# Seven half-width products in place of eight for two thirds of an expert layer's blocks (linear attention, then hash-routed experts)

## The chip, the cores and the metric

One core of one Trainium2 chip runs the whole kernel in one launch. The metric is the device time of that launch in microseconds (us), the median of several runs. Every matrix and every product is float32. The engines are named as the profile names them: PE (matrix products; PEld is its loading of weights), DVE (vector), ACT (activation), POOL (general, here the one that scatters rows) and SP (issues the loads).

## The reference

```python
def _attn_ref(q, k, v, beta):                      # (4, 8, 768, 48)
    k_n = k / (np.linalg.norm(k, axis=-1, keepdims=True) + 1e-06)
    state = np.zeros((B, H, D, D))
    for t in range(S):
        kt, vt, bt = (k_n[:, :, t], v[:, :, t], beta[:, :, t, None])
        y[:, :, t] = np.einsum('bhd,bhde->bhe', q[:, :, t], state)
        v_old = np.einsum('bhde,bhd->bhe', state, kt)
        state = state + bt[:, :, :, None] * np.einsum('bhd,bhe->bhde', kt, vt - v_old)
    return y

def _moe_ref(x, token_ids, w1, w2):                # x: y as (3072, 384); w1 (8, 384, 1024); w2 (8, 1024, 384)
    expert_idx = token_ids * np.int64(2654435761) % np.int64(E)
    for e in range(E):
        mask = expert_idx == e
        h = np.maximum(x[mask] @ w1[e], 0.0)
        out[mask] = h @ w2[e]
    return out
```

## The kernel before

**First part, the attention.** The 768 tokens of a sequence are taken in 24 chunks of 32, for all 32 heads at once. `chunk(c)` is the recurrence; DVE inverts a triangular matrix for each group of four chunks (`inverse`). A list scheduler (`order()`) with estimated costs sets the order of this part's instructions. At the end of a chunk ACT copies the finished rows out of PSUM into `x_sb` (L695), and POOL scatters them to a DRAM scratch, sorted by expert.

**Second part, the experts.** The experts are sorted by their number of tokens and called e0 to e7 here (the largest is e0). Each has a fixed width, `WIDTHS` = 424, 424, 392, 392, 380, 380, 366, 366 columns (tokens); what is over goes through a loop at the end that runs as often as the data ask. 288 columns of e0 (`EARLY`) are computed ahead, at the end of the first part; its other 136 (`LATE`) open the second part's loop. This part's order is the order of the code (`tc.manual_schedule()`), engine by engine.

- `fetch(e)` and `weights(e)` issue the loads on SP's queue: rows from the scratch, `w1` and `w2` of an expert (1536 KB each). `w_pool2` has three buffers of each weight; e4 takes e0's place (`w_first`).
- `turn(e, i)`: DVE transposes the rows in 32x32 blocks, with a stride of three, to `xT`, whose 384 input features lie as three blocks of 128 (index `co` or `i`).
- `gemm1` (L1186): the first product. For each of 8 blocks of 128 hidden features (`fo`), three matrix products (one for each `co`) of the full width add up in one PSUM bank; ACT (L1189) and DVE (L1191) take turns at clearing negative values on the way to `h_sb`.
- `turned` (L1216): the second product of e0 to e6. For each of three output blocks `i`, eight products (one for each `fo`); the weights are `w2[:, fo, i::CO]`, so every third column. DVE transposes the bank to `o_sb` (L1219), and `scatter` (L1224) sends it out, one indirect DMA of POOL for each 32 tokens.
- `direct` (L1199): the second product of e7, with tokens on the partitions, in three pieces of 122 tokens; then a copy (L1203) and a scatter (L1205).

A float32 product shows up in the trace as two passes, each with a weight load and a matmul: a row with x48 stands for 24 products. e0's late 136 columns use a copy of its `w2` with contiguous columns (`w2_runs`, made by ACT at L1252); all the other `turned` products load strided weights.

## Time and profile before

| what | value |
|---|---|
| median of 3 runs | 483.76 us (483.18 to 486.18) |
| the profiled execution: time, span in the trace | 486.72 us, 485.1 us |
| PE busy | 440.3 us (91%), 6544 matmuls |
| PEld busy | 335.5 us (69%) |
| DVE busy | 249.5 us (51%) |
| ACT busy | 170.5 us (35%) |
| POOL busy | 175.0 us (36%) |
| mean granted TensorE clock | 0.952 of full speed |

Busy time is a share of the whole span, which has two very different parts. The first ends at about 221 us; the second is read by itself. The profiled execution's time is 1.62 us more than its span, and 2.96 us above the median of the runs.

### The profile page before, as it was taken

What the parts mean: (1) busy time and instruction counts of PE and PEld (TensorE: products, weight loads), DVE (VectorE), ACT (ScalarE), POOL (GpSimd) and SP (SyncE); (2) the same over time, 40 slices, a digit from 0 to 9 for tenths busy, and PEclk for the clock granted to TensorE, in tenths of its full rate; (3) what the DMA queues carried; (4) which work ended last, traced back from release to release, by engine and by line L of the source; (5) the groups of instructions that cost most, each with busy time, mean ns of one, the idle gap of its engine ahead of it and who ended that gap; (6) DMA issues with size and microseconds to landing.
All of it is one profiled execution on the core that took longest, in us unless ns stands there. A gap on an engine that the chain in (4) does not pass through costs nothing. (4 is left out here: it accounts for less than half of the span.)

```text
span 485.1 us, 15906 instructions
## 1 busy us (share of the span) xinstructions
PE 440.3 (91%) x6544; PEld 335.5 (69%) x6544; DVE 249.5 (51%) x903; ACT 170.5 (35%) x361; POOL 175.0 (36%) x231
## 2 busy tenths in 40 slices
PE   6798898989988977789999999999999999999991
PEld 4675787877767876677896665766767767677650
DVE  6799899999999799981222121221212112121100
ACT  3569876858866566455000001001000010000100
POOL 9671323214131251532056007427054170541710
PEclk8759799989998899899999999999999999999997
DMA  8994646556573373544998237064090460000100
GB/s 128 148 154 110 113 86 131 108 102 122 105 133 83 97 163 80 106 168 114 317 311 251 94 59 282 22 201 157 10 321 29 100 255 3 24 23 7 38 32 16
DMA packets 98009, 58.28 MB, mean 120 GB/s; under 512 B 84262, under 2 KB 91953, under 8 KB 97168
## 3 DMA queue, kind: packets, MB, share of 16 engines
q1 hardware_dynamic: 88640, 39.67, 34.8%
q0 software_dynamic: 8016, 17.27, 13.2%
q8 instruction: 52, 0.85, 0.8%
q10 hardware_dynamic: 1280, 0.32, 0.3%
q14 instruction: 21, 0.17, 0.1%
HBM read 44.51 MB, written 10.65 MB: 114 GB/s over the span
## 5 line engine op out<-in xcount | busy, mean ns | idle before, releaser
L1224 POOL DMA_INDIRECT out_dram<-o_sb,idx x81 | 79.3, 979 | 123.1 <-DVE o_sb L1219 100.4
L1186 PE MATMUL h_ps<-xT,w_sb 128*128 128x392 f32 (+3 forms) x288 | 94.5, 488 | 0.0
L1189 ACT ACTIVATE h_sb<-h_ps 128x392 f32<-128x392 f32 (+4 forms) x32 | 14.9, 466 | 211.4 <-PE h_ps L1186 211.4
L1186 PEld LDWEIGHTS h_ps<-xT,w_sb 128*128 128x128 f32 x288 | 54.6, 190 | 38.2 <-issue 7.6
L1216 PE MATMUL o_ps<-h_sb,w_sb 128*128 128x392 f32 (+3 forms) x240 | 79.6, 491 | 0.0
L1216 PEld LDWEIGHTS o_ps<-h_sb,w_sb 128*128 128x128 f32 x240 | 60.3, 251 | 18.8 <-issue 0.2
L1191 DVE TENSOR_SCALAR h_sb<-h_ps 128x392 f32<-128x392 f32 (+4 forms) x32 | 16.9, 527 | 95.9 <-PE h_ps L1186 95.9
L700 POOL DMA_INDIRECT x_scratch<-x_sb,slot x24 | 25.9, 1078 | 104.1 <-ACT x_sb L695 34.1
L1219 DVE STREAM_TRANSPOSE o_sb<-o_ps 128x384 f32<-128x384 f32 (+4 forms) x24 | 16.1, 669 | 84.7 <-PE o_ps L1216 84.7
L571 DVE TENSOR_TENSOR U<-U,tmp 128x30 f32<-128x30 f32 (+9 forms) x180 | 58.1, 323 | 0.0
L567 DVE TENSOR_TENSOR tmp<-U,Ni 128x30 f32<-128x30 f32 (+9 forms) x180 | 57.9, 322 | 0.1
L602 PE MATMUL bank<-S,KQ 128*32 128x96 f32 x1472 | 38.6, 261 | 4.7 <-ACT S L748 4.0
L563 DVE SCALAR_TENSOR_TENSOR U<-U,Ni 128x1 f32<-128x1 f32 (+30 forms) x186 | 42.4, 228 | 0.2
L748 ACT ACTIVATE S<-psS 48x768 f32<-48x768 f32 x43 | 34.6, 806 | 19.0 <-PE psS L670 15.6
L602 PEld LDWEIGHTS bank<-S,KQ 128*32 128x32 f32 x1472 | 33.4, 117 | 8.7 <-ACT S L748 5.8
L670 PE MATMUL psS<-W,K 32*112 32x96 f32 x736 | 26.9, 275 | 8.7 <-ACT W L660 5.5
L641 PE MATMUL bank<-W,MT 64*64 64x48 f32 x768 | 30.3, 231 | 2.0 <-issue 1.5
L670 PEld LDWEIGHTS psS<-W,K 32*112 32x112 f32 x736 | 22.2, 178 | 12.1 <-ACT W L660 7.4
L641 PEld LDWEIGHTS bank<-W,MT 64*64 64x64 f32 x768 | 26.8, 145 | 4.9 <-issue 2.4
L506 POOL DMA_DIRECT2D Tz<-TU x24 | 17.6, 741 | 29.3 <-ACT Tz L951 12.7
L335 POOL DMA_DIRECT2D Q<-in_q_dram x40 | 23.0, 583 | 6.1 <-PE early L370 4.2
L489 ACT ACTIVATE MT<-GQ,kmask 128x256 f32<-128x256 f32 x48 | 22.3, 512 | 0.0
(167 smaller groups left out, 588.5 us busy)
## 6 DMA issues: line engine op xcount, KB each, us to landing
w_sb<-in_moe_w_dram SPq DMA_DIRECT2D x12, 1536.0 KB
V<-in_v_dram SPq DMA_DIRECT2D x96, 48.0 KB
K<-in_k_dram SPq DMA_DIRECT2D x89, 48.0 KB
Q<-in_q_dram SPq DMA_DIRECT2D x56, 48.0 KB
xr<-x_scratch SPq DMA_DIRECT2D x16, 145.5 KB
Tz<-TU POOLq DMA_DIRECT2D x24, 96.0 KB, 3.3
Q<-in_q_dram POOLq DMA_DIRECT2D x40, 48.0 KB, 4.4
w_first<-in_moe_w_dram POOLq DMA_DIRECT2D x3, 512.0 KB, 5.0
```

The source lines that it names most:

```text
L335: eng].dma_start(out=dst[quarter(b)],
L563: nc.vector.scalar_tensor_tensor(out=U[:, n, 0:n], in0=U[:, j, 0:n], scalar=Ni[:, j, n:n + 1], in1=U[:, n, 0:n], op0=ALU.mult, op1=ALU.add)
L567: nc.vector.tensor_tensor(t, U[:, j:n, 0:n].to_broadcast([P, m, n]), Ni[:, j, n + 1:, None].to_broadcast([P, m, n]), op=ALU.mult)
L571: nc.vector.tensor_tensor(U[:, n + 1:, 0:n], U[:, n + 1:, 0:n], t, op=ALU.add)
L602: nc.tensor.matmul(res[quarter(b), u], lhsT=KQ[:, u, a, quarter(b)], rhs=S0[:, b, u].rearrange("p r d -> p (r d)"), start=(a == 1 and u == ...
L641: nc.tensor.matmul(to[rows, h], lhsT=lhsT(rows, h), rhs=rhs[rows, h], start=(first and h == 0), stop=True, skip_group_check=True, tile_pos ...
L670: nc.tensor.matmul(late["S"][0:DP + D, b, 2 * D * u:2 * D * u + 2 * D], lhsT=K4[quarter(b), u].rearrange("p r d -> p (r d)")[:, 0:DP + D], ...
L700: put = nc.gpsimd.indirect_dma_start(out=x_dram[:, :], out_offset=bass.IndirectOffsetOnAxis(ap=slot[:, c:c + 1], axis=0), in_=x_sb.rearran ...
L748: put = nc.scalar.activation(S1[half(r), :, :, r], new[half(r), :, :, r], ACT.Copy)
L1186: nc.tensor.matmul(h_ps[:, :width], lhsT=w1_sb[:, co, fo * P:(fo + 1) * P], rhs=xT[:, co, :width], start=(co == 0), stop=(co == CO - 1))
L1216: nc.tensor.matmul(os_ps[i][:, 0:width], lhsT=w2_sb[:, fo, i::CO] if runs is None else runs[:, fo, i], rhs=h_sb[:, fo, 0:width], start=(fo ...
L1224: scat = nc.gpsimd.indirect_dma_start(out=out_q, out_offset=bass.IndirectOffsetOnAxis(ap=of[:, k:k + 1], axis=0), in_=o_sb[:, k], in_offse ...
```

## The change

For e1 to e7 two of the three blocks of the first product's contraction (`co` 0 and 1) are no longer multiplied out as 2 x 2 block products of half the columns. The weights are cut in 2 x 2 blocks (hidden features f and f+4 against `co` 0 and 1), the tokens in two halves, and each set of eight half-width products is replaced by seven, of sums and differences of the blocks (Winograd's form of Strassen's method): DVE makes the sums of weights and columns beforehand (`sums1`), and DVE and ACT join the products out of four half banks. The third block (`co` 2) is multiplied as before, in halves. The same is done in the second product of e1 to e5, with output blocks 0 and 1 against hidden blocks f and f+4 (`seven2`, `sums2_weights`, `sums2_columns`); output block 2 keeps its eight full-width products there. e0's products, e6's second and e7's second product keep their form; e7's are put in another order, and its result is copied in two halves, by ACT and by DVE.

In the loop e's first product now stands ahead of (e-1)'s second, and e0's late second product behind e1's first. The sums for an expert stand on DVE one stage ahead. `w_pool2` has two buffers; e0's place takes e3 and e6. The load of an expert's `w1` is issued three experts ahead, as soon as its place is free, that of its `w2` two ahead. In the first part the rows are laid out differently: ACT's copy to `x_sb` reads PSUM with a stride of three, and DVE's transposes to `xT` read contiguous rows.

```diff
-                x_sb[:, :, 0:DQ], flat_y.rearrange("p (q y) -> p q y", q=QN), ACT.Copy, scale=-1.0))
+                x_sb[:, :, 0:DQ].rearrange("p q (i r) -> p q i r", i=CO),
+                flat_y.rearrange("p (q r i) -> p q i r", q=QN, i=CO), ACT.Copy, scale=-1.0))
...
-    with tc.tile_pool(name="w_pool2", bufs=3) as w_pool2, \
+    with tc.tile_pool(name="w_pool2", bufs=2) as w_pool2, \
...
+        banks = [ps_m.tile([P, BANK], F32, name=f"bank{i}") for i in range(8)]
+        os_ps, hs_ps, t_ps = banks[0:3], banks[3:6], banks[6]
+        HF, HB, HC = F // 2, FO // 2, CAP // 2
+        two = itertools.cycle([(banks[i], banks[i + 1]) for i in range(0, 8, 2)])
...
+        def sums_of_weights(s, a11, a12, a21, a22):
+            return [plus(s[0], a21, a22), minus(s[1], s[0], a11), minus(s[2], a11, a21),
+                    minus(s[3], a12, s[1])]
+
+        def sums_of_columns(t, b11, b12, b21, b22):
+            return [minus(t[0], b12, b11), minus(t[1], b22, t[0]), minus(t[2], b22, b12),
+                    minus(t[3], b21, t[1])]
...
+        def seven1(e, h_sb, others):
...
+            def first(f):
+                used[f], part[f] = next(two), next(parts)
+                al, be, de, ep = halves_of(used[f], n)
+                blk = slice(f * P, f * P + P)
+                mm(al, a(0, f), x[:, 0, 0:n], True)
+                mm(be, s[1][:, blk], t[1][:, 0:n])
+                mm(ep, s[2][:, blk], t[2][:, 0:n], True)
+                mm(de, s[0][:, blk], t[0][:, 0:n])
+                mm(de, a(2, f + HB), x[:, 2, n:2 * n])
+                p0, p1 = (p[:, 0:n] for p in part[f])
+                nc.scalar.copy(p1, al)
+                run([plus(p0, p1, be), plus(p1, p0, ep), plus(h_sb[:, f + HB, n:2 * n], p1, de)])
+
+            def second(f):
...
+                mm(al, a(1, f), x[:, 1, 0:n])
+                mm(al, a(2, f), x[:, 2, 0:n])
+                mm(ep, a(1, f + HB), t[3][:, 0:n])
+                mm(ep, a(2, f + HB), x[:, 2, 0:n])
+                mm(de, s[3][:, blk], x[:, 1, n:2 * n])
+                mm(de, s[4][:, blk], x[:, 2, n:2 * n])
+                p0 = part[f][0][:, 0:n]
+                nc.scalar.activation(h_sb[:, f, 0:n], al, ACT.Relu)
+                run([plus(h_sb[:, f + HB, 0:n], p0, ep)])
+                nc.scalar.activation(h_sb[:, f + HB, 0:2 * n], h_sb[:, f + HB, 0:2 * n], ACT.Relu)
+                run([plus(h_sb[:, f, n:2 * n], p0, de)])
+                nc.scalar.activation(h_sb[:, f, n:2 * n], h_sb[:, f, n:2 * n], ACT.Relu)
+
+            for what, f, k in ((first, 0, 2), (first, 1, 1), (first, 2, 1), (second, 0, 1),
+                               (first, 3, 1), (second, 1, 1), (second, 2, 1)):
+                what(f)
+                run(others, k)
+            run(others)
+            second(3)
+
+        def seven2(e, h_sb, o_sb, befores, others):
...
+            for fo in range(FO):
+                mm(third[:, 0:2 * n], of_out(w2[:, fo], 2), h_sb[:, fo, 0:2 * n], fo == 0)
+            for f in range(HB):
+                mm(al, of_out(w2[:, f], 0), h_sb[:, f, 0:n], f == 0)
+            for f in range(HB):
+                mm(be, s[1][:, f], t[1][:, f, 0:n])
...
+            run(befores)
+            nc.scalar.copy(oT[2][:, 0:2 * n], third[:, 0:2 * n])
+            turn_out(e, o_sb, 2)
+            nc.scalar.copy(p1, al)
+            run([plus(p0, p1, be)])
+            run(others, 1)
+            run([plus(p1, p0, ep)])
+            run(others, 1)
+            run([plus(oT[1][:, n:2 * n], p1, de)])
+            run(others)
+            for f in range(HB):
+                mm(al, of_out(w2[:, f + HB], 0), h_sb[:, f + HB, 0:n])
+            for f in range(HB):
+                mm(ep, of_out(w2[:, f + HB], 1), t[3][:, f, 0:n])
...
+            for e in range(1, E - 1):
+                hs[e] = m_h.tile([P, FO, CAP], F32, name="h_sb")
...
+                seven1(e, hs[e], others)
...
+                    turns_of_rows(e + 1)
+                    o_sb = m_o.tile([P, NB_MAX, DQ], F32, name="o_sb")
+                    others = sums2_columns(e, hs[e]) if e < E - 2 else []
+                    seven2(e - 1, h_sb, o_sb, sums1(e + 1),
+                           (sums2_weights(e) if e < E - 2 else []) + others[:2])
+                    del others[:2]
+                    scatter(idx[e - 1], o_sb, range(NBS[e - 1]))
+                if e + 2 < E:
+                    weights2(e + 2)
+                if e + 3 < E:
+                    fetch(e + 3)
+                    weights1(e + 3)
...
```

PE, at e2's last first-product blocks and the second product that follows them, before (`h_ps` and `o_ps` are PSUM banks; x3 and x8 count products, of 392 columns):

```order
L1186 MATMUL h_ps_4962<-xT,w_sb 128x392 x3
L1186 MATMUL h_ps_4963<-xT,w_sb 128x392 x3
L1216 MATMUL o_ps_4958<-h_sb,w_sb 128x392 x8
L1216 MATMUL o_ps_4959<-h_sb,w_sb 128x392 x8
L1216 MATMUL o_ps_4960<-h_sb,w_sb 128x392 x8
```

The same place on PE now: `second(3)` of e2's first product, then e1's second product (`h_first` holds its sums of weights, `h_sums` its sums of columns):

```order
L1169 MATMUL bank_4964<-xT,w_sb 128x196 x2
L1169 MATMUL bank_4965<-x_sum_4978,w_sb 128x196
L1169 MATMUL bank_4965<-xT,w_sb 128x196
L1169 MATMUL bank_4965<-xT,w_sum_4969 128x196
L1169 MATMUL bank_4965<-xT,w_sum_4970 128x196
L1169 MATMUL bank_4960<-h_sb,w_sb 128x424 x8
L1169 MATMUL bank_4958<-h_sb,w_sb 128x212 x4
L1169 MATMUL bank_4958<-h_sums,h_first 128x212 x4
L1169 MATMUL bank_4959<-h_sums,h_first 128x212 x8
L1169 MATMUL bank_4958<-h_sb,w_sb 128x212 x4
L1169 MATMUL bank_4959<-h_sums,w_sb 128x212 x4
L1169 MATMUL bank_4959<-h_sb,h_first 128x212 x4
```

Half-width products stand where full-width ones stood, and the last three rows add to half banks that DVE and ACT must first have read.

DVE during e2's second product, before (`xT<-xr` turns the next expert's rows, `o_sb<-o_ps` the results):

```order
L1191 TENSOR_SCALAR h_sb<-h_ps_4963 128x392
L1166 STREAM_TRANSPOSE xT<-xr 128x416
L1219 STREAM_TRANSPOSE o_sb<-o_ps_4958 128x416
L1166 STREAM_TRANSPOSE xT<-xr 128x416
L1219 STREAM_TRANSPOSE o_sb<-o_ps_4959 128x416
```

DVE during e1's second product now (`w_sum` and `x_sum` above the `o_sb` row are e3's, for the first product that follows; `w_sum_4971` and later are e2's, for its second product; `part` and `oT` join e1's):

```order
L1155 TENSOR_TENSOR w_sum_4970<-w_first 128x512
L1286 STREAM_TRANSPOSE o_sb<-oT_4990 128x448
L1158 TENSOR_TENSOR part_4980<-part_4981,bank_4958 128x212
L1158 TENSOR_TENSOR w_sum_4971<-w_sb 128x512
L1158 TENSOR_TENSOR part_4981<-part_4980,bank_4959 128x212
L1155 TENSOR_TENSOR w_sum_4972<-w_sum_4971,w_sb 128x512
L1158 TENSOR_TENSOR oT_4989<-part_4981,bank_4959 128x212
L1155 TENSOR_TENSOR w_sum_4973<-w_sb 128x512
```

The reads of `bank` that release PE's last three rows now stand behind three transposes and nine sums, and between further sums.

## Rows read from the trace of the kernel before

**Rows 1.** PE in order of time: start us, us, line, operation; x48 is 24 products

```profile
200.65 1.14 PE L641 MATMUL pair<-R,Tz 64*64 64x48 f32 x32 [1.96 <-DVE Tz L499]
...
233.57 11.95 PE L1216 MATMUL o_ps<-h_first,w_first 128*128 128x288 f32 x48 [0.60 <-issue]
245.35 5.72 PE L1186 MATMUL h_ps<-xT,w_first 128*128 128x136 f32 x48
250.91 5.72 PE L1216 MATMUL o_ps<-h_sb,w_runs 128*128 128x136 f32 x48
256.47 17.24 PE L1186 MATMUL h_ps<-xT,w_sb 128*128 128x424 f32 x48
273.55 17.24 PE L1216 MATMUL o_ps<-h_sb,w_sb 128*128 128x424 f32 x48
290.63 15.96 PE L1186 MATMUL h_ps<-xT,w_sb 128*128 128x392 f32 x48
306.43 15.96 PE L1216 MATMUL o_ps<-h_sb,w_sb 128*128 128x392 f32 x48
...
429.87 14.92 PE L1216 MATMUL o_ps<-h_sb,w_sb 128*128 128x366 f32 x48
444.63 14.92 PE L1186 MATMUL h_ps<-xT,w_sb 128*128 128x366 f32 x48
```

**Rows 2.** Busy time by stage: PE, PEld, DVE, ACT, POOL; then clock, DMA, GB/s

```profile
180.00:200.00 20.00, 14.98 (x512) 13.09 (x500) 19.89 (x79) 12.42 (x30) 5.01 (x7) 1.00 0.35 83
...
233.50:245.40 11.90, 11.83 (x49) 11.81 (x50) 1.14 (x2) 0.00 (x0) 0.00 (x0) 1.00 1.11 322
245.40:256.40 11.00, 11.00 (x97) 11.00 (x96) 4.58 (x12) 1.13 (x4) 7.86 (x8) 1.00 0.78 289
...
290.00:322.00 32.00, 32.00 (x99) 21.45 (x98) 6.39 (x11) 1.99 (x4) 13.71 (x14) 1.00 0.44 137
```

**Rows 3.** PE's weight loads by form, 270 to 486 us: busy us, mean ns

```profile
L1216 PEld LDWEIGHTS o_ps<-h_sb,w_sb 128*128 128x128 f32 x240 | 60.3, 251 | 18.8 <-issue 0.2
L1186 PEld LDWEIGHTS h_ps<-xT,w_sb 128*128 128x128 f32 x249 | 47.3, 190 | 32.1 <-issue 1.7
...
L1199 PEld LDWEIGHTS o_ps<-w_sb,h_sb 128*122 128x122 f32 x48 | 8.9, 185 | 6.6
```

**Rows 4.** DVE by form, 300 to 486 us: busy us, mean ns of one

```profile
L1166 DVE STREAM_TRANSPOSE xT<-xr 128x384 f32<-128x384 f32 x12 | 7.9, 658 | 0.0
...
L1191 DVE TENSOR_SCALAR h_sb<-h_ps 128x392 f32<-128x392 f32 x6 | 3.4, 566 | 20.1 <-PE h_ps L1186 20.1
```

**Rows 5.** DVE by form, 200 to 262 us

```profile
L1191 DVE TENSOR_SCALAR h_sb<-h_ps 128x136 f32<-128x136 f32 x4 | 1.2, 299 | 4.1 <-PE h_ps L1186 4.1
```

**Rows 6.** DVE in order of time, 212 to 290 us

```profile
212.07 0.38 DVE L769 TENSOR_TENSOR rt<-rt,iota_f 128x216 f32<-128x216 f32 x1
212.49 0.38 DVE L769 TENSOR_TENSOR rt<-rt,rt 128x216 f32<-128x216 f32 x1
```

**Rows 7.** ACT by form, 200 to 262 us

```profile
L1252 ACT COPY w_runs<-w_first 128x384 f32<-128x384 f32 x8 | 5.1, 709 | 2.3 <-DMA x_scratch<-x_sb,slot 2.3
...
L695 ACT ACTIVATE x_sb<-bank 128x384 f32<-128x384 f32 x4 | 2.0, 491 | 2.6 <-PE bank L641 1.5 <-issue 1.1
...
L1189 ACT ACTIVATE h_sb<-h_ps 128x136 f32<-128x136 f32 x4 | 1.1, 284 | 17.6 <-PE h_ps L1186 17.6
```

**Rows 8.** ACT in order of time, the last chunks of the first part

```profile
217.84 0.55 ACT L632 ACTIVATE R<-bank 128x192 f32<-128x192 f32 x2 [0.57 <-PE bank L602]
```

**Rows 9.** SP's queue in order of time: the issue of e1's `w1`

```profile
230.05 0.36 SPq L80 DMA_DIRECT2D w_sb<-in_moe_w_dram  x1
```

**Rows 10.** The end of the kernel, in order of time

```profile
475.11 0.48 ACT L1203 COPY last_o<-o_ps 122x384 f32<-122x384 f32 x1 [9.83 <-PE o_ps L1199]
475.86 0.98 POOL L1205 DMA_INDIRECT out_dram<-last_o,last_i  x1 [4.07 <-POOLq L1286]
```

More of the change, by code (lines that the diff above doesn't have):

```diff
@@ new lines, with minus, plus @@
+        w2_runs = h_all[:, 0:FO * CO * P].rearrange("p (o i d) -> p o i d", o=FO, i=CO)
+        parts = itertools.cycle([[m_l.tile([P, HC], F32, name=f"part{i}{k}") for k in range(2)]
+                                 for i in range(4)])
+        oT = [m_l.tile([P, NB_MAX * TB], F32, name=f"oT{i}") for i in range(CO)]
+        def minus(out, a, b):
+            return lambda: nc.vector.tensor_tensor(out, a, b, op=ALU.subtract)
+        def plus(out, a, b):
+            return lambda: nc.vector.tensor_tensor(out, a, b, op=ALU.add)
@@ new lines, in seven2 @@
+        def seven2(e, h_sb, o_sb, befores, others):
+            w2, s, t, n = w_tiles[e][1], w2_sums[e % 2], h_sums, WIDTHS[e] // 2
+            pair, (third, _) = next(two), next(two)
+            al, be, de, ep = halves_of(pair, n)
+            p0, p1 = (p[:, 0:n] for p in next(parts))
+            for fo in range(FO):
[5 more added lines that the diff above has]
+            for f in range(HB):
+                mm(ep, s[2][:, f], t[2][:, f, 0:n], f == 0)
+            for f in range(HB):
+                mm(de, s[0][:, f], t[0][:, f, 0:n])
+            run(befores)
[8 more added lines that the diff above has]
+            run(others)
+            for f in range(HB):
+                mm(al, of_out(w2[:, f + HB], 0), h_sb[:, f + HB, 0:n])
+            for f in range(HB):
+                mm(ep, of_out(w2[:, f + HB], 1), t[3][:, f, 0:n])
+            for f in range(HB):
+                mm(de, s[3][:, f], h_sb[:, f + HB, n:2 * n])
+            nc.scalar.copy(oT[0][:, 0:n], al)
+            run([plus(oT[1][:, 0:n], p0, ep)])
+            turn_out(e, o_sb, 1)
+            run([plus(oT[0][:, n:2 * n], p0, de)])
+            turn_out(e, o_sb, 0)
@@ L1228, in scatter, with weights1, weights2, turns_of_rows @@
                 tc.add_to_no_dep_group("scatters", scat.ins)
[L1230 to L1236 removed]
+        def weights1(e):
+            w1 = moe_w1[bass.ds(regs[1][e], 1)].rearrange("o d f -> (o d) f")
+            home = w_tiles[0][0] if e % 3 == 0 else w_pool2.tile([P, CO, F], F32, name="w1_sb")
+            nc.sync.dma_start(out=home, in_=w1.rearrange("(p co) f -> p co f", p=P))
+            w_tiles[e] = home, None
+        def weights2(e):
+            w2 = moe_w2[bass.ds(regs[1][e], 1)].rearrange("o f d -> (o f) d")
+            home = w_tiles[0][1] if e % 3 == 0 else w_pool2.tile([P, FO, DIN], F32, name="w2_sb")
+            nc.sync.dma_start(out=home, in_=w2.rearrange("(fo p) d -> p fo d", p=P))
+            w_tiles[e] = w_tiles[e][0], home
+        def turns_of_rows(e):
+            for i in range(CO):
+                turn(e, i)
+            places(e)
         with tc.manual_schedule():
@@ L1240 @@
             fetch(1)
-            weights(1)
+            weights1(1)
+            weights2(1)
+            turns_of_rows(0)
+            n_ov = nc.values_load(ov_i[0:1, NOV:NOV + 1], min_val=0, max_val=NOV)
+            fetch(2)
+            weights1(2)
+            weights2(2)
             w1_sb, w2_sb = w_tiles[0]
-            for i in range(CO):
-                turn(0, i)
-            places(0)
             o_sb = m_o.tile([P, NB_MAX, DQ], F32, name="o_sb")
+            turns_of_rows(1)
+            soon = sums1(1)
+            run(soon, 3)
             for i in range(CO):
                 turned(w2_sb, first["h"], o_sb, i, EARLY, 0)
+                run(soon, 3 if i < CO - 1 else None)
             scatter(idx_first, o_sb, range(EB))
-            w2_runs = m_l.tile([P, FO, CO, P], F32, name="w2_runs")
-            for fo in range(FO):
-                nc.scalar.copy(w2_runs[:, fo], w2_sb[:, fo].rearrange("p (d i) -> p i d", i=CO))
+            fetch(3)
+            for t in oT:
+                nc.vector.memset(t, 0.0)
             nc.vector.memset(last_i, BIG)
@@ L1286 @@
+            e = E - 2
+            o_sb = m_o.tile([P, NB_MAX, DQ], F32, name="o_sb")
+            os_ps = [next(two)[0] for _ in range(CO)]
+            for i in range(CO):
+                turned(w_tiles[e][1], hs[e], o_sb, i, WIDTHS[e], 0)
+            scatter(idx[e], o_sb, range(NBS[e]))
+            hs[e + 1] = m_h.tile([P, FO, CAP], F32, name="h_sb")
+            seven1(e + 1, hs[e + 1], [])
+            direct(w_tiles[e + 1][1], hs[e + 1])
         with tc.For_i(0, n_ov, 1) as it:
@@ L1315 @@
             gemm1(w1_sb, xT, h_sb, P)
-            direct(w2_sb, h_sb, 0, P, to[:, 0:1], False)
+            for fo in range(FO):
+                nc.tensor.matmul(os_ps[0][:, 0:DIN], lhsT=h_sb[:, fo, 0:P], rhs=w2_sb[:, fo, :],
+                                 start=(fo == 0), stop=(fo == FO - 1))
+            last(os_ps[0], P, 0, to[:, 0:1])
 _INS = ['q', 'k', 'v', 'beta', 'moe_token_ids', 'moe_w1', 'moe_w2']
```

150 lines of the change are left out of this document (94 added, 56 removed).

## The prediction

> **What bounds the kernel now.** I read the stages first, then PE in order of time, then the loads and the helpers by form. From 245 us on PE is busy all the time, at a granted clock of 1.00, the 2.4 GHz level; DVE is busy 6.4 us of 32 and ACT 2.0 [rows 2]. PE's rows follow each other without a gap [rows 1], so in the second part a column of PE work saved is time saved, as long as nothing new holds PE up. The length of a pass comes from the starts: 48 passes of 392 columns take 306.43 - 290.63 = 15.80 us, 329.2 ns each; of 424 columns 17.08 us, 355.8 ns; of 366 columns 14.76 us, 307.5 ns; of 136 columns 5.56 us, 115.8 ns [rows 1]. All four lie on 0.833 ns a column plus 2.5 ns. By that line 380 columns take 319.2 ns, and halves take 179.2 (212 columns), 165.8 (196), 160.8 (190) and 155.0 ns (183).
>
> **First products of e1 to e7.** A first product was 24 full-width products, 48 passes. Now each of four blocks has 5 products in `first` and 6 in `second`, so 44 of half width, 88 passes: 88 x 179.2 = 15.77 us for 17.08; 14.59 for 15.80 (e2, e3); 14.15 for 15.32 (e4, e5); 13.64 for 14.76 (e6, e7). Gains: 1.31 + 2 x 1.21 + 2 x 1.17 + 2 x 1.12 = 8.3 us.
>
> **Second products of e1 to e5.** Eight full products stay (16 passes), 28 half ones follow (56 passes). 16 x 355.8 + 56 x 179.2 = 15.73 us for 17.08 (e1); 14.55 for 15.80 (e2, e3); 14.11 for 15.32 (e4, e5). Gains: 1.35 + 2 x 1.25 + 2 x 1.21 = 6.3 us. The columns together: **14.6 us**. e0's, e6's second and e7's second products keep their passes.
>
> **Weight loads under shorter passes.** Loads overlap the pass before. A contiguous load is recorded with 190 ns [rows 3], yet 96 passes of 136 columns go at 115.8 ns with PEld busy throughout [rows 1, 2]: at least 74 ns of the record don't hold up the next. Half passes with contiguous weights, at 155 ns or more, are therefore covered by a row. Strided loads are not: recorded with 251 ns [rows 3], and the shortest pass that covers them in this trace is one of 288 columns, 11.78 us / 48 = 245.4 ns, at most 3 ns over the line [rows 1]. Now 12 half products of each `seven2` (the `al` and `ep` ones that read `w2` itself), 24 passes, have strided weights. At best they cost nothing. At worst each is as long as 245 ns: 24 x (66 + 2 x 79 + 2 x 84) ns = 9.4 us. In between: 122 columns are recorded with 185 ns, 128 with 190 [rows 3], so some 0.83 ns a column and 83 ns of latency; taken off 251 that leaves an estimate of 168 ns, above the half passes by 2 ns (196) and 7 ns (190): 24 x (2 x 2 + 2 x 7) = 0.4 us. I take 0.4, since the 136-column row shows that the recorded duration overstates a load.
>
> The Trainium skill, TensorE: Matmul & The Clock Gate, The mechanism, says that a weight load overlaps matmuls in flight only when their row groups differ; all loads here use all rows. By it every added pass would pay its load. The trace disagrees: passes of 115.8 ns have no room for a load of that kind [rows 1].
>
> **The sums on DVE.** Costs from rows: 392 columns 566 ns, 136 columns 299 [rows 4, 5], so 1.04 ns a column; two dependent ones of 216 columns start 0.42 us apart [rows 6]. So about 0.36 to 0.40 us for a half-width one, 0.64 for 512 columns, 0.66 for a transpose of 384 [rows 4]. For an expert of 29 us of PE work: joining in `seven1` 20 x 0.37 = 7.4; sums of h 8 x 0.53 = 4.2; `sums1` 5 x 0.64 + 4 x 0.34 = 4.6; sums of `w2` 4 x 0.66 = 2.6; joining in `seven2` 5 x 0.38 = 1.9; six transposes 4.0: 24.7 us, 86% of 14.59 + 14.11 = 28.7. DVE was a fifth busy; it becomes nearly as full as PE, but hides, if nothing has to come too early. ACT gets 16 operations of about 0.35 to 0.5 us in `seven1` and three in `seven2`, some 8 us of 29 [rows 7], and hides.
>
> The tightest place is the second half of `seven2`. PE runs straight from `seven1(e)` into it and reaches the `al` rows after 5.27 + 32 x 0.166 = 10.6 us, the `ep` rows 1.3 us later, at 11.9 (196 columns). Before the `ep` rows DVE must have read the `de` half. Its queue from the same moment: last joins of `seven1` 0.9, three transposes and places 2.1, `sums1` 4.6 (8.2 with the transpose that follows), join, sum, join, sum 2.1: about 10.3; the `de` products end at 10.6, the join then ends near 11.2. That is 0.7 us ahead of PE. `second(0)` of `seven1` comes 5.0 us after its start and needs joins that end about 3.2 after it; the banks of the last `seven2` are free 1 us after PE leaves it, and are needed 3.3 after. So I cost DVE's new work at nothing, plus 0.5 us for small waits; its cover is 0.7 us an expert.
>
> **Start of the second part.** `seven1(1)` stands where e0's late second product stood, at 250.9. It needs e1's `w1`, issued at 230.05 [rows 9]: 1536 KB at 322 GB/s [rows 2] are 4.9 us; with the rows ahead of it in the queue that is about 237. DVE then has `sums1(1)`, 4.6 us, between the three transposes of e0's early columns, the last ready at 245.5 [rows 1]: done by 246. SP's queue carries the same loads in the same order there. Later a `w1` is issued a stage and more ahead of its sums (one took 5 us), and one waiting for its place holds only loads for later experts: nothing. POOL's 12 scatters an expert, about 1 us each, were covered by 32 us and are by 29.
>
> **First part.** The copy to `x_sb` takes 491 ns from contiguous PSUM [rows 7]; no row shows ACT reading PSUM with a stride. The nearest is the strided copy of `w2` from SBUF with the same 384 columns, 709 ns [rows 7]: 218 ns more, 24 times, 5.2 us if all of it were on the path. It is not: up to 200 us DVE is the full engine (19.9 of 20 us) [rows 2], the chunk at 200.65 waits 1.96 us for DVE anyway [rows 1], and in the last chunks ACT idles 0.57 us behind that copy [rows 8]. I take 0.3 us; the ends are 0 and 5.2. Transposes with contiguous reads can only shorten DVE's list there, at no gain.
>
> **End.** The last copy shrinks from 0.48 [rows 10] to about 0.33 us (half the columns): 0.1 us gained, left out.
>
> **Sum.** 14.6 - 0.4 - 0.5 - 0.3 = 13.4 us. The profiled span goes from 485.1 to 471.7, that execution from 486.72 to 473.3. It lay 2.96 us above the median of its runs; against the median, 483.76, I predict **470.4 us**.
>
> **Rivals.**
> 1. *Strided loads uncovered*: passes of 245 ns in `seven2`. For it: 251 ns recorded. Against: the overstatement seen at 136 columns. Gain 13.4 - 9.0 = 4.4, 479.4 us. 0.08.
> 2. *DVE late in `seven2`*: with DVE's operations a quarter longer (half-read strided sums, banks shared with PE), its 10.3 us become 12.9, the `ep` rows wait about 1.4 us, five times: 7 us, 477.4. For it: only 0.7 us of cover. Against: the durations are this trace's. 0.11.
> 3. *DVE becomes the bound; slower than before.* 25 joins an expert read a bank that PE is filling just then, which no row of before shows. At 0.8 us each instead of 0.37 DVE needs 24.7 + 10.8 = 35.5 us for 31.1 before: +4.4 in five stages, 22 us, 506. It decides from about 0.63 us a join. 0.04.
> 4. *The copy to `x_sb` on the path*: 5.2 us, 475.3. Against: DVE's full row. 0.04.
> 5. *Loads in series*: the change has 7 x 40 + 5 x 24 = 400 more passes; at the 107 ns of a load's columns (128 x 0.83) 42.8 us more, so 42.8 - 14.6 = 28 slower, 512. Against: the 136-column row. 0.01. This is what the page's rule would do here.
> 6. *It doesn't do what it says*: small waits and loads together eat the columns, within 1% of before, 482. 0.04.
>
> The forecast has 0.68, own range 468.3 to 473. A measurement of this kernel tells a change from none from about 1%, 4.8 us. Faster by more than that are the forecast, 2 and 4, and half of 1: 0.87; within it half of 1 and 6: 0.08; slower 3 and 5: 0.05. The range for 8 in 10 runs from 468.3 (no load exposed, no wait) to 477.5, the price of 2.
>
> **What the changed profile would show.** PE's starts: `seven1` of 392 columns 14.6 us long, `seven2` of 392 columns 14.55, without idle time before their parts; if `al` and `ep` rows with `w2` itself take more than 166 ns a pass where rows with sums don't, loads are exposed. DVE busy about 24 us of each 29 and 0.36 to 0.40 us a join; a wait of PE for `oT` or `part` rows means that DVE was late. `x_sb` copies near 0.7 us with `fetch(0)` still issued near 225.5. The forecast is wrong if PE shows idle time in each expert, or if passes leave the line of 0.833 ns a column.

## The result, and the profile after

Measured: 470.81 us (median of 4 runs, 469.36 to 477.04) beside 483.47 us of the kernel before; ratio 0.9717, 95% interval 0.9667 to 0.9768. The predicted time was 470.4. Later timings of the same kernel, on two chips, came out the other way, 1.016 and 1.031 of the kernel before; they are in the experiments below. This part reads the first timing's trace.

The profiled execution took 469.36 us with a span of 467.8. From its page, busy time and share of each engine:

```profile
PE 419.3 (90%) x6944; PEld 372.4 (80%) x6944; DVE 348.8 (75%) x1161; ACT 201.1 (43%) x465; POOL 181.9 (39%) x232
```

DVE, a fifth busy in the second part before [rows 2], is now busy for 146.3 of its 240.0 us (61%; 74% from e2's first product to e5's second), and still not the bound. PE in order of time (start, busy time, line, count); the rows answer to the starts in [rows 1]:

```profile
227.81 11.94 PE L1380 MATMUL bank<-h_first,w_first 128*128 128x288 f32 x48 [0.60 <-issue]
239.59 5.72 PE L1336 MATMUL bank<-xT,w_first 128*128 128x136 f32 x48
245.15 0.52 PE L1169 MATMUL bank<-xT,w_sb 128*128 128x212 f32 x2
...
260.92 5.72 PE L1380 MATMUL bank<-h_sb,h_sums 128*128 128x136 f32 x48
266.49 0.60 PE L1169 MATMUL bank<-xT,w_sb 128*128 128x196 f32 x2
...
281.19 7.30 PE L1169 MATMUL bank<-h_sb,w_sb 128*128 128x424 f32 x24
...
297.36 0.49 PE L1169 MATMUL bank<-xT,w_first 128*128 128x196 f32 x2
...
311.95 1.49 PE L1169 MATMUL bank<-h_sb,w_sb 128*128 128x392 f32 x4
...
327.14 0.48 PE L1169 MATMUL bank<-xT,w_sb 128*128 128x190 f32 x2
...
413.58 14.94 PE L1380 MATMUL bank<-h_sb,w_first 128*128 128x366 f32 x48
428.36 0.47 PE L1169 MATMUL bank<-xT,w_sb 128*128 128x183 f32 x2
...
442.02 15.64 PE L1360 MATMUL bank<-w_sb,h_sb 128*122 128x384 f32 x48
```

Differences of such starts give the stages, in us:

| stage | foreseen | first timing | unedited, second timing | unedited, third | a break behind each scatter |
|---|---|---|---|---|---|
| `seven1` of e1 | 15.77 | 15.77 | 20.68 | 19.12 | 15.77 |
| `seven1` of e2 / e3 | 14.59 | 14.70 / 14.59 | 14.70 / 14.59 | 14.70 / 14.59 | 14.70 / 14.59 |
| `seven2` of e1 | 15.73 | 16.17 | 16.17 | 16.17 | 16.18 |
| `seven2` of e2 / e3 | 14.55 | 15.19 / 15.20 | 15.18 / 15.19 | 15.30 / 18.34 | 15.18 / 15.19 |
| `seven2` of e4 / e5 | 14.11 | 14.85 / 14.42 | 14.85 / 14.42 | 18.96 / 14.43 | 14.85 / 14.42 |
| `seven1` of e7 | 13.64 | 13.66 | 28.97 | 30.00 | 13.66 |

In the first timing the half products of `seven1` lie on the line of 0.833 ns a column plus 2.5 ns. `seven2` is 0.44, 0.64, 0.65, 0.74 and 0.31 us longer than its columns, 2.8 us together where 0.9 was foreseen. From e0's early second product (227.81; 233.57 before [rows 1]) to the end of the span the second part takes 240.0 us, and before 251.6: 11.6 us won. The rest of the 12.7 us between the medians, 1.1 us, is left for the first part. The two profiles show 5.8 us there (227.81 and 233.57), but every later profile started that product somewhere else, from 230.5 to 242.2 us, so nothing can be told of it.

Where the 2.8 us are is seen in the second half of e2's `seven2`, PE and DVE in order of time (the last bracket is idle time and what ended it):

```profile
320.48 0.36 DVE L1158 TENSOR_TENSOR part<-part,bank 128x196 f32<-128x196 f32 x1 [1.26 <-ACT part L1265]
320.76 0.85 DVE L1158 TENSOR_TENSOR h_first<-w_first 128x512 f32<-128x512 f32 x1
322.42 1.47 PEld L1169 LDWEIGHTS bank<-h_sb,w_sb 128*128 128x128 f32 x8
322.58 1.55 PE L1169 MATMUL bank<-h_sb,w_sb 128*128 128x196 f32 x8
322.78 0.36 DVE L1158 TENSOR_TENSOR part<-part,bank 128x196 f32<-128x196 f32 x1 [1.18 <-PE bank L1169]
323.06 0.87 DVE L1155 TENSOR_TENSOR h_first<-h_first,w_first 128x512 f32<-128x512 f32 x1
323.83 0.36 DVE L1158 TENSOR_TENSOR oT<-part,bank 128x196 f32<-128x196 f32 x1
...
324.25 1.48 PEld L1169 LDWEIGHTS bank<-h_sums,w_sb 128*128 128x128 f32 x8 [0.36 <-DVE oT L1158]
324.25 1.73 PE L1169 MATMUL bank<-h_sums,w_sb 128*128 128x196 f32 x8
```

The join at 322.78 reads `ep`, whose products had ended 1.3 us earlier, but `de` lies in the same bank, and DVE starts only when the last `de` product is through (322.58 is PE's next start). It is the program that makes it wait: the semaphore by which PE releases the join rises in the trace with the last `be` product (320.11) and with the last `de` product (322.76), and not behind `ep`. Whether the chip would let DVE read one half while PE fills the other is not shown. Behind that join one sum of `w2` (0.87 us) still stands ahead of the join that frees `de`, and PE's `ep` rows wait for it. This happens in e1 to e4, not in e5, whose `seven2` has no such sums beside it.

### The profile page after: what moved, and what is told of

It is laid out like the page before. It is cut to its first block, busy times and chain, and to the rows that moved or that the text cites. A ratio compares the mean times of both kernels' runs of the same rounds, so it can differ in the third digit from the quotient of the medians.

```text
span 467.8 us, 17087 instructions
## 1 busy us (share of the span) xinstructions
PE 419.3 (90%) x6944; PEld 372.4 (80%) x6944; DVE 348.8 (75%) x1161; ACT 201.1 (43%) x465; POOL 181.9 (39%) x232
## 5 line engine op out<-in xcount | busy, mean ns | idle before, releaser
L1388 POOL DMA_INDIRECT out_dram<-o_sb,idx x81 | 86.0, 1061 | 107.6 <-DVE part L1158 59.4
L1158 DVE TENSOR_TENSOR h_sb<-part,bank 128x196 f32<-128x196 f32 (+3 forms) x84 | 27.3, 352 | 21.2 <-PE bank L1169 20.1
L1169 PE MATMUL bank<-xT,w_sb 128*128 128x190 f32 (+3 forms) x200 | 42.8, 328 | 0.0
L1158 DVE TENSOR_TENSOR part<-part,bank 128x196 f32<-128x196 f32 (+3 forms) x66 | 23.2, 351 | 25.3 <-ACT part L1221 8.3
L1169 PEld LDWEIGHTS bank<-xT,w_sb 128*128 128x128 f32 x200 | 34.3, 190 | 0.2
L1169 PE MATMUL bank<-h_sb,w_sb 128*128 128x380 f32 (+5 forms) x128 | 33.7, 416 | 0.0
L1221 ACT COPY part<-bank 128x196 f32<-128x196 f32 (+3 forms) x28 | 8.8, 315 | 55.7 <-PE bank L1169 55.7
L1169 PE MATMUL bank<-x_sum,w_sum 128*128 128x196 f32 (+3 forms) x168 | 32.0, 326 | 0.0
L1169 PEld LDWEIGHTS bank<-h_sb,w_sb 128*128 128x128 f32 x128 | 27.9, 254 | 5.1
L1236 ACT ACTIVATE h_sb<-h_sb 128x392 f32<-128x392 f32 (+3 forms) x28 | 14.7, 525 | 34.6 <-DVE h_sb L1158 34.6
```

The costliest lines, as they stand in the source:

```text
L1158: return lambda: nc.vector.tensor_tensor(out, a, b, op=ALU.add)
L1169: nc.tensor.matmul(out, lhsT=lhsT, rhs=rhs, start=start, stop=True, skip_group_check=True)
L1388: scat = nc.gpsimd.indirect_dma_start(out=out_q, out_offset=bass.IndirectOffsetOnAxis(ap=of[:, k:k + 1], axis=0), in_=o_sb[:, k], in_offse ...
```

## The experiments

Each ran beside the kernel before, on one of two chips; ratios are against that, with 95% intervals. The second timing shared its chip with the runs on the order of the joins, on weights in one run and on the rows of x, and later with the last two with breaks; all others, the third timing among them, ran on the other.

**The changed kernel again, twice (no edit).**

> The changed kernel once more, as the yardstick for the runs beside it: 470.8 us. Its second products of five experts should again be longer than their columns by about 0.45, 0.65, 0.65, 0.75 and 0.3 us. If the first part (PE's start of the early first products of the first expert, 215.3 us in the profile of after, 221.1 in that of before) moves by more than a microsecond between two profiles of this one kernel, the difference of the two profiles there is mostly from run to run.

> The changed kernel, unedited, a third time. Its second timing gave 496.9 us where the first gave 470.8, and the two traces differ in the second part at two places alone: the first products of e1 take 20.7 us instead of 15.8, those of e7 29.0 instead of 13.7, with PE's instructions starting 0.70 us apart from 446.6 to 460.6, until POOL's run of 24 scatters is over. If that is a state which only some executions or chips have, a third run can show either 470.8 or 496.9; if it is the rule, 496.9. Between the two nothing is foreseen.

Measured: 496.85 us beside 489.47, ratio 1.0157 (1.0108 to 1.0206), and 505.15 beside 492.81, ratio 1.0307 (1.0228 to 1.0385): slower than before. The table above shows where. In the second timing every stage agrees with the first to 0.02 us but two, `seven1` of e1 and of e7, which are 4.9 and 15.3 us longer; together they are all of the 20.2 us that its second part takes more. In the third `seven2` of e3 and e4 are longer as well. PE of the second timing, in the first products of e7:

```profile
446.01 0.47 PE L1169 MATMUL bank<-xT,w_sum 128*128 128x183 f32 x2
446.32 0.32 PE L1169 MATMUL bank<-xT,w_sb 128*128 128x183 f32 x1
447.33 0.32 PE L1169 MATMUL bank<-xT,w_sb 128*128 128x183 f32 x1 [0.69 <-issue]
448.73 0.47 PE L1169 MATMUL bank<-x_sum,w_sum 128*128 128x183 f32 x2 [1.09 <-issue]
451.52 0.32 PE L1169 MATMUL bank<-x_sum,w_sum 128*128 128x183 f32 x1 [2.32 <-issue]
452.23 0.46 PE L1169 MATMUL bank<-x_sum,w_sum 128*128 128x183 f32 x1 [0.39 <-issue]
453.63 0.47 PE L1169 MATMUL bank<-x_sum,w_sum 128*128 128x183 f32 x1 [0.93 <-issue]
```

"issue" means that PE waited for nothing that the profile shows; loads and products start 0.70 us apart or a multiple of it (446.63, 447.33, 448.02, 448.73). Busy time and, behind the five engines, the granted clock, of that trace:

```profile
427.60:446.60 19.00, 19.00 (x84) 16.44 (x82) 3.14 (x6) 0.31 (x1) 14.67 (x15) 1.00 0.11 36
446.60:460.60 14.00, 3.45 (x10) 2.37 (x10) 1.04 (x3) 0.31 (x1) 8.81 (x9) 0.70 0.10 33
460.60:484.20 23.60, 23.58 (x84) 16.71 (x83) 5.01 (x16) 5.03 (x16) 1.96 (x2) 0.89 0.05 17
```

Ten passes in 14 us; the granted clock is at the 1.2 GHz level from 452.2 to 465.9 us, after PE has stood idle. DMA is a tenth busy, so no load is late. What is busy is POOL, with an unbroken run of 24 scatters (e5's and e6's, 427.6 to 458.1), one each 1.28 us, and PE's passes follow each other again 2.5 us after the last. In `seven1` of e1 it is ACT that starts late, beside the 9 scatters of e0's early rows (247.2 to 258.5):

```profile
251.48 0.28 ACT L1339 ACTIVATE h_sb<-bank 128x136 f32<-128x136 f32 x1 [0.47 <-PE bank L1336]
254.34 0.28 ACT L1339 ACTIVATE h_sb<-bank 128x136 f32<-128x136 f32 x1 [2.58 <-PE bank L1169]
257.18 0.34 ACT L1221 COPY part<-bank 128x212 f32<-128x212 f32 x1 [2.55 <-PE bank L1169]
260.11 0.57 ACT L1221 COPY part<-bank 128x212 f32<-128x212 f32 x2 [2.60 <-PE bank L1169]
```

PE had left the last of the first products' banks at 251.84 (246.12 and 5.72 us), and still ACT reads it at 254.34, and then takes 2.8 to 2.9 us from each operation to the next. The brackets name PE, whose product had long ended; what came late is not its work. The semaphore with which PE tells ACT is next recorded at 254.32, 0.02 us ahead of ACT's start, where in the first timing it rises 0.01 us behind each product. So either the signal was late or its record is missing.

In the third timing ACT and DVE start late beside e2's scatters (340.1 to 357.4) too, and in e3's `seven2` PE then waits 2.6 us for DVE:

```profile
353.67 0.52 ACT L1236 ACTIVATE h_sb<-h_sb 128x380 f32<-128x380 f32 x1 [4.04 <-issue]
364.92 1.72 PE L1169 MATMUL bank<-h_sb,w_first 128*128 128x196 f32 x8 [2.58 <-DVE part L1158]
```

Do PE's instructions come late from memory? The trace has the transfers of blocks of instructions, 16,384 bytes each, in a queue (q8) that in the second timing gets one each 125 to 128 of PE's passes from 361 us on. One starts at 432.16, in the middle of the run of scatters, and takes 0.93 us; the next starts at 473.66, 128 passes later. PE's stall begins 67 passes behind the first of the two. DMA queues (packets, MB, share) from 427.6 to 446.6 us, and then from 446.6 to 460.6:

```profile
q8 instruction: 1, 0.02, 0.3%
```

```profile
q0 software_dynamic: 320, 0.46, 10.0%
```

The second stretch, the stall, has packets of the scatters' queue alone. So no block of PE's instructions was under way in the stall, and by this trace none came late; what hands them on from there to PE is not in it.

**A break behind each scatter**, beside the third timing:

```
                 in_=o_sb[:, k], in_offset=None, ...)
+            nc.gpsimd.memset(pause, 0.0)       # 128x384
```

> The changed kernel with a clearing of 128x384 values on POOL (0.44 us) behind each scatter, so that scatters no longer follow each other at 1.27 us but at 1.7 to 1.8. Theory: while POOL issues scatters without a break, instructions reach PE and ACT only every 0.70 us once what they hold is used up; with breaks they get through, and the first products of e1 and e7 take 15.8 and 13.7 us: 20 us less than the unedited kernel beside it, if that shows the stalls, and no change of more than 1 us if it doesn't. Rival: it hangs on the place in the program (the same ten passes of e7's first products in every run), not on POOL: the same 20.7 and 29.0 us. Other rival: scatters in any number do it, and as the runs of scatters get longer by the breaks, the stalls get longer too.

Measured: 475.41 us beside 492.81, ratio 0.9681 (0.9621 to 0.9741), where the unedited kernel beside it has 1.0307. POOL's and then PE's rows in the first products of e7:

```profile
437.59 0.97 POOL L1389 DMA_INDIRECT out_dram<-o_sb,idx  x1 [0.16 <-issue]
438.56 0.43 POOL L1392 MEMSET pause<- 128x384 f32 x1
439.16 0.97 POOL L1389 DMA_INDIRECT out_dram<-o_sb,idx  x1 [0.17 <-issue]
```

```profile
443.75 0.47 PE L1169 MATMUL bank<-xT,w_sb 128*128 128x183 f32 x2
444.06 1.09 PE L1169 MATMUL bank<-x_sum,w_sum 128*128 128x183 f32 x6
444.99 1.09 PE L1169 MATMUL bank<-xT,w_sb 128*128 128x183 f32 x6
```

The scatters come every 1.57 us, all stages return to those of the first timing (last column of the table), and the second part takes 476.9 - 236.7 = 240.2 us, 0.2 more than there. So the stalls hang on POOL's scatters following each other without a break, not on the place in the program, and not on there being scatters. The rivals fall.

**A break behind each fourth scatter** (`if k % 4 == 3` ahead of the same line).

> The changed kernel with the clearing on POOL behind each fourth scatter alone: runs of four scatters at 1.27 us, then a break of 0.44 us. Theory that any break lets the held instructions through: no stalls, the first products of e1 and e7 take 15.8 and 13.7 us, 0.968 of the kernel before as with a break behind each. Rival, that the mean pace of the scatters counts (1.38 us here, 1.35 in the runs of scatters that showed no stalls beside a busy DVE, 1.26 in those that did): nearly no stalls either. Other rival, that a break must follow each scatter: stalls stay, above 0.99 of the kernel before.

Measured: 490.41 us beside 489.12, ratio 1.0043 (1.0012 to 1.0075). `seven1` of e1 takes 17.64 us, of e7 27.44. Four scatters at 1.28 us and one break are a mean of 1.34 to 1.36 us, and PE stalls; so the theory that any break will do falls. The mean pace doesn't tell the cases apart either: runs of scatters beside a busy DVE, in which single scatters stretch to 1.2 to 1.3 us, came to 1.36 in the second timing without a stall of PE's stages beside them, and to 1.36 in the third, where e3's and e4's `seven2` are 3.1 and 4.1 us longer. Between a break behind each and one behind each fourth the bound wasn't looked for.

**First products only**: the second products whole again.

```
-                    seven2(e - 1, h_sb, o_sb, sums1(e + 1), ...)
+                    for i in range(CO):
+                        turned(w_tiles[e - 1][1], h_sb, o_sb, i, WIDTHS[e - 1], 0)
+                        if i == 0: run(sums1(e + 1))
```

> The changed kernel with the second products of the second to sixth expert whole again (24 full-width products each, no sums of w2 or of h, no joins behind them); first products with seven half-width products stay. By the columns it gives back 6.3 us and, if the 2.8 us of waits and strided loads belong to the second products alone, drops those: 470.8 + 6.3 - 2.8 = 474.3 us. Rival: the waits come from the DVE work that the first products brought (sums of w1, joins), and go to another place: up to 477 us.

Measured: 517.94 us beside 488.62, ratio 1.0601 (1.0539 to 1.0664), far outside both. With less on DVE the scatters of all experts run unbroken (1.28 us each), and now nearly every expert stalls: `seven1` of e3 to e5 17.7, 18.3 and 17.7 us (columns 14.6, 14.2, 14.2), the second products that follow 18.6 to 19.1 (columns 15.8 and 15.3), e7 28.0. All stages together are 42 us over their columns. To take these off would leave the columns, whatever the 2.8 us are, so the run doesn't test the account of `seven2`; the one second product without a stall, e1's, takes its columns (17.09 us for 17.08). It tells more of the stalls: they now fall on passes of full width too.

**Order of the joins in `seven2`.**

```
-            run(others, 1)
+            run(others, 2)
             run([plus(p1, p0, ep)])
-            run(others, 1)
             run([plus(oT[1][:, n:2 * n], p1, de)])
```

> Theory: in each second half-width product the ep rows wait because one sum of w2 (0.86 us) stands on DVE between the join that reads ep and the join that frees de, and the first of these can't start before the last de product. With both sums ahead of the ep join DVE does them in its 1.2 us of idle time: the waits (0.44 us in four of the five experts, 1.8 us in all) go, 469.0 us, and the first ep pass takes 173 ns and not 335. Rival: DVE's queue as a whole is late there (the cover of 0.7 us is used up by the transposes, the sums of w1 and the copies on ACT); then the two joins only swap places with the sums, the waits stay, 470.8 us.

Measured: 495.71 us, ratio 1.0124 (1.0069 to 1.018), beside the second timing: the stalls in both hide what was asked. By the stages: `seven2` of e1 and e3 15.73 and 14.75 us for 16.17 and 15.19, of e2 and e4 15.30 and 15.42 for 15.18 and 14.85. Two of four got the 0.44 us; in the other two ACT's copy of the third column came 8.6 and 7.5 us after the stage's start (5.5 in the first timing), so that both sums no longer fitted ahead of the join, and PE's `ep` rows waited for it (0.6 us idle in e4, ended by `oT` on DVE). Inconclusive alone.

**Joins, breaks and e6 in halves**: the edit above, the breaks behind each scatter, and `seven2` for e6 too, its sums beside e5's. The sums of e6's h stand ahead of e5's last `ep` rows in it, which multiply by them: this part of e5's output is not the reference's, and PE waits there for the sums.

> The changed kernel with three edits: the clearings behind the scatters on POOL (475.4 us alone, 0.968 of the kernel before), both sums of w2 ahead of the ep join, and the second product of e6 with half-width products too, where its full-width one stood, its sums of w2 and h on DVE beside the second product of e5. Theory: no stalls of PE's and ACT's instructions; second products of e1 to e4 0.44 us shorter each (1.8), that of e6 13.8 us instead of 14.77 (1.0): 0.962 of the kernel before, 472.6 us beside 475.4. If ACT's late copies in the first run of this order came from POOL's scatters, the gain of 0.44 must now show in all four of these experts; if they came from the order itself, it shows in two of them again. Rival: the eight sums of h don't fit beside e5's second product (4.4 us ahead of its last joins), and e6's waits for them: over 14.8 us, nothing gained there.

Measured: 480.13 us beside 489.12, ratio 0.9836 (0.9775 to 0.9897), without stalls, on the other chip than the first run with breaks. `seven2` of e1 to e4 15.73, 14.75, 14.75 and 14.42 us, shorter by 0.44, 0.44, 0.44 and 0.43: in all four, so the theory of the joins stands, and ACT's late copies came with the unbroken scatters, not from the order. In e2 the join reads `ep` as soon as the bank is free, and PE's `ep` rows follow their `al` rows without a wait:

```profile
323.75 0.85 DVE L1158 TENSOR_TENSOR h_first<-w_first 128x512 f32<-128x512 f32 x1
324.64 0.87 DVE L1155 TENSOR_TENSOR h_first<-h_first,w_first 128x512 f32<-128x512 f32 x1
325.57 1.55 PE L1169 MATMUL bank<-h_sb,w_sb 128*128 128x196 f32 x8
325.77 0.36 DVE L1158 TENSOR_TENSOR part<-part,bank 128x196 f32<-128x196 f32 x1 [0.26 <-PE bank L1169]
326.17 0.36 DVE L1158 TENSOR_TENSOR oT<-part,bank 128x196 f32<-128x196 f32 x1
...
326.96 1.56 PE L1169 MATMUL bank<-h_sums,w_sb 128*128 128x196 f32 x8
```

`seven2` of e6 takes 14.04 us for 14.77, but e5's 20.34 for 14.42 because of that wait; it is why the kernel is over the 472.6 us expected. Its time is therefore no measure of the best form; joins and breaks in one kernel that computes everything were not run.

**Joins and e6, placed behind e7's first products, no breaks.**

> The order of the joins as in the experiment on it (469.0 us by that theory), and the second product of the seventh expert with half-width products too, placed like the others behind the first products of the eighth. Columns: 48 x 307.5 ns = 14.76 us become 16 x 307.5 + 56 x 155 = 13.60, less 24 x 18 ns = 0.4 of strided loads: 0.7 us gained, 468.3 us. Rival: its 12 scatters (1.06 us each on POOL, 12.7 us) now start only about 15 us before the end, and the last rows' scatters queue behind them: then up to 1 us later, 469.3, and POOL shows no idle time before the last scatters.

Measured: 481.94 us beside 488.62, ratio 0.9854 (0.98 to 0.9908). `seven1` of e7 takes 13.65 us: e6's scatters no longer stand beside it, and e5's, alone, are stretched by a busy DVE. That of e1 still stalls (22.0 us). `seven2` of e6 is 14.06 us, 0.71 won, as worked out. The rival happened too: 15 scatters without idle time end at 475.2 us, 5.9 us after PE, where 2.1 us were between them in the first timing.

**Weights in one run of columns in `seven2`** (`w2[:, f, 0:P]` and the like for `of_out(w2[:, f], 0)`).

> In the second half-width products the al and ep products take their weights from 128 neighbouring columns of w2, not from every third; they multiply by other columns of w2 than the reference. Theory: a load with a stride holds a pass up to 173 ns; 24 passes an expert of 196, 190 and 212 columns then get shorter by 7, 13 (14) and 0 ns: about 0.9 us in all, 469.9 us, the wait ahead of the ep rows stays, and the al and ep passes return to 0.833 ns a column plus 2.5. Rival: strided loads are the whole of the 2.8 us beyond the columns, and DVE's late join is only their consequence: 468.0 us. Other rival: loads are hidden and 173 ns comes from something else: 470.8 us.

Measured: 494.43 us, ratio 1.0112 (1.0066 to 1.0158), stalls as beside it; the stages tell. `seven2` gets shorter by 0.07, 0.18, 0.20, 0.26 and 0.29 us, 1.0 together, and the wait ahead of the `ep` rows stays. PE in e5's `seven2`, first timing and then this kernel:

```profile
409.52 1.55 PE L1169 MATMUL bank<-h_sb,w_sb 128*128 128x190 f32 x8
410.90 1.56 PE L1169 MATMUL bank<-h_sums,w_sb 128*128 128x190 f32 x8
```

```profile
414.57 1.45 PE L1169 MATMUL bank<-h_sb,w_sb 128*128 128x190 f32 x8
415.85 1.45 PE L1169 MATMUL bank<-h_sums,w_sb 128*128 128x190 f32 x8
```

With a stride (410.90 - 409.52) / 8 = 172.5 ns a pass, without 160. The theory holds, the other two fall.

**Strided loads in the kernel before** (`None` for `None if e else w2_runs`).

> The kernel before, with one edit: the late second product of the first expert (48 passes of 136 columns, 5.56 us) reads w2 with its stride of three, where it read the copy w2_runs; the copies on ACT stay. If a strided load holds a pass up to 173 ns: 48 x (173 - 115.8) = 2.7 us longer, 486.2 us. Rival 1 of the prediction (245 ns a pass): 6.2 us longer, 489.7 us. Rival 5 (loads in series): with or without a stride a pass would be at least the columns and a load, 113 + 107 = 220 ns, and the row of 115.8 ns has already spoken against it. Loads hidden: 483.5 us.

Measured: 490.15 us beside 488.62, ratio 1.0007 (0.9965 to 1.0048); 2.7 us are 0.6%, which the ratio can't tell apart from none, and the trace can:

```profile
245.85 5.72 PE L1186 MATMUL h_ps<-xT,w_first 128*128 128x136 f32 x48
251.41 8.54 PE L1216 MATMUL o_ps<-h_sb,w_first 128*128 128x136 f32 x48
259.78 1.59 PE L1186 MATMUL h_ps<-xT,w_sb 128*128 128x424 f32 x4
```

(259.78 - 251.41) / 48 = 174.4 ns a pass, where the first products with 136 columns and loads from one run take 115.8. That is the bound of a strided load by itself: 2.8 us more, not 6.2.

**Four sums more on DVE** (`* (5 if e > 2 else 1)` on the last sum of `sums1`).

> The changed kernel with the last sum of w1 done five times over (four more sums of 512 columns, 0.72 us each, 2.9 us of DVE work) ahead of the joins of each of the five second half-width products. If the cover there were the 0.7 us that the prediction worked out, PE would wait 2.2 us more in each: 11 us, 481.8 us. By the profile of after DVE idles 1.2 us ahead of the ep join: 1.7 us more in each of four and less in the fifth, about 7.5 us, 478.3 us. If DVE has far more room (rival 2 void): under 2 us, 472.5 us.

Measured: 504.22 us beside 488.62, ratio 1.0297 (1.0242 to 1.0352), again with the stalls of e1 and e7. By the stages `seven2` of e2, e3 and e4 is longer by 1.4, 1.6 and 1.8 us, of e1 not at all and of e5 by 0.15. The four sums take 2.9 us (they start 0.72 us apart), so the cover was 1.1 to 1.5 us here, in a run in which ACT was late as well, and over 2.7 for e1 and e5: nearer to the second figure expected than to the 0.7 us of the prediction.

**Rows of x as before.** The copy to `x_sb`, the turns and the flattening as before the change.

> The changed kernel with the rows of x stored as before the change (the copy to x_sb reads PSUM in order, the turns of rows read every third column). Rival 4 of the prediction, that the copy's strided reading costs time: the copies get shorter and the time falls below 470.8 us, up to 5.2 us. My forecast's 0.3 us: 470.5. Theory now, since the copies took 490 ns in both profiles: no gain there; the turns on DVE go from 0.55 to 0.66 us, three an expert, 0.33 us in the queue ahead of the ep join, where DVE idles 1.2 us: hidden, 470.8 us. If the first part gained about 1 us by the shorter transposes, it is 471.8 us and PE starts the early first products about 1 us later.

Measured: 495.21 us, ratio 1.012 (1.0078 to 1.0161), beside 1.0157: no difference that can be told. The copies take 492 ns, in the kernels before and after 490 and 490; the second part 260.3 us and the unedited one 260.2. Rival 4 is void, and the new layout gave nothing that these runs can tell.

## Why the prediction was right, and where not

The mechanism was right: passes saved are time saved, in the first timing and in the kernel with a break behind each scatter. Two terms were too small, one foreseen cost did not come, and what scatters can do to the other engines was missing.

**The columns** are right to 0.1 us in each `seven1` without stalls, and with them the step that contiguous loads are covered at 155 ns and more. Rival 5, loads in series, is void: 48 first products of 136 columns still take 5.56 us (239.59 to 245.15 above).

**Strided loads** were taken as an estimate of 168 ns a pass, 0.4 us in all; they measure 173 to 174.5 and 1.0 us. Right in kind, too small by 0.6. Rival 1 at 245 ns is void.

**DVE in `seven2`**, foreseen with 0.5 us of small waits under a cover of 0.7, cost 1.76 us (the 0.44 us that the other order gave back, four times). 1.0 and 1.8 are the 2.8 us over the columns. The step that failed is a detail of the queue: the prediction let the `ep` join run in order behind the sums, when in this program it waits for the bank that `ep` shares with `de`; and it took 0.66 us for a sum of `w2`, where those that read with a stride take 0.85 to 0.87, and 0.64 for a sum of 512 columns, where its own line of 1.04 ns a column gives 0.69. The cover as a length was underrated (1.2 us idle there and 1.3 before it), and still PE waited, because the idle time lay ahead of a join that couldn't start. Rival 2 is this in small. Rival 3 is void: joins take 0.34 to 0.37 us, though PE is filling the bank's neighbour.

**The copy to `x_sb`**: 0.3 us foreseen, none measured.

**The sum**: the second part won 11.6 us, against 13.7 foreseen for it (14.6 - 0.4 - 0.5), and the first part, which cannot be told from run to run, gave 1.1 us between the medians of the first timing, where a loss of 0.3 was foreseen. That 470.8 lies so near to 470.4 is luck to that extent. It is luck, too, that the first timing had no stalls: in the second and third timing the same kernel is slower than before, for a reason that no rival of the prediction has.

**What the prediction had wrong about POOL** is the sentence that its scatters were covered by 32 us and are by 29. Their duration is covered; what comes with them for the other engines was put at nothing. The first timing shows 24 scatters at 1.28 us (416.1 to 446.7) beside e7's first products without any stall, the two later ones show the stalls at the same place, and no trace of the kernel before shows one, although its scatters are as unbroken and its trace with the one edit is from one of those chips.

Why unbroken scatters hold PE and ACT up is not shown. One idea is a store of instructions that isn't filled meanwhile, and that half-width passes empty sooner, at an instruction pair each 0.16 us and not each 0.33. For it: in the run with first products only PE stood 71 to 79 passes after the start of the runs of scatters of e1 to e6, in the second timing 82, and the 12 scatters of e6 before (445.8 to 460.9) span 50 passes. Against it: the kernel before runs 90 passes of 136 columns, at 115.8 ns each, beside 9 unbroken scatters (246.4 to 257.7) without a stall, the first timing runs 142 passes beside 24, and the blocks of PE's instructions came in time.

The Trainium skill, Runtime: NRT & Kernel Launch, Instruction fetch mechanics, says that an engine's sequencer fetches its instructions in blocks of 16 KiB by a DMA queue of its own while it executes, and that crossing a block costs little. The page of the profile after lists 55 packets and 0.90 MB in such a queue, 16.4 KB each, which agrees; so do the blocks at 432.16 and 473.66 in the second timing, neither of which is at the stall.

**Left open**: why the first timing has no stalls. Both chips of the later timings show them, and the kernel before is 5 to 9 us slower there than beside the first; which chip that was is not in its records. The traces differ in one more thing. In the two of the first timing nearly every rise of the semaphores of PE, ACT and DVE is recorded beside the second part's scatters (all of 146 before, 368 of 370 after). In the later ones many are missing just there: 130 of 310 in the second timing, 48 of 137 in the kernel before with its one edit, 105 of 395 in the run with a break behind each scatter, which has no stalls; away from the scatters 8 of 289, 12 of 112 and 2 of 204. So on those chips records of the trace go missing beside scatters, too. Every timed run of the changed kernel has a span and a clock of a trace on record; whether the stalls would come without tracing, and whether it is the chip or the place of the program in its memory, can't be told from these runs.

## What to carry to other kernels

Cutting passes in half buys columns, and doubles the instructions that an engine must be fed in a microsecond: look what else is issued without a break beside it, and try a short pause behind each of a row of scatters if PE's rows show idle time that ends with "issue". A join of one half of a PSUM bank can be made to wait, as here, until the products into the other half have ended, so look which product releases it, and put work that needs no bank ahead of such a join, not behind it. A ratio from one timing can be of the other sign in the next, as here; stages by PE's starts tell which part of a change holds everywhere.

## What was not expected of the hardware

- In the later timings, on two chips, PE's instructions start 0.70 us apart or more beside unbroken scatters on POOL (one each 1.28 us) once some 70 to 90 passes have gone, and ACT's operations 2.9 us; a clearing of 0.43 us behind each scatter ends it, one behind each fourth doesn't. In the first timing 142 passes beside 24 such scatters show nothing of it.
- A load of 128x128 weights with a stride of three holds a pass at 173 to 174.5 ns, whether it streams 136, 190 or 196 columns; from one run of columns, passes of 115.8 ns have no wait.
- A strided read of PSUM by ACT costs nothing: 128x384 in 490 ns either way. On DVE a 512-column sum of weights takes 0.68 to 0.75 us, and 0.85 to 0.87 with the stride of three in SBUF.
- POOL's scatters take 0.98 us alone and 1.2 to 1.3 beside some of DVE's work. With less work on DVE, where none is stretched, nearly every expert stalls; in the second timing none does beside stretched ones, in the third two do.
